# Layer 1 of a tail group by seven block products, with the last sum in two banks and the last row block's store on two queues

## The chip, the cores and the metric

The kernel runs on one core of one Trainium2 chip. The metric is device time in microseconds (us), the median of several executions. A profile is taken of one further execution; its span leaves out a little of what the timed execution counts. All runs here are with a granted TensorE clock of 0.99 or more over the span.

Two kinds of number are used. **Timed** numbers scatter: the kernel before had medians from 313.76 to 314.52 us in the rounds of these experiments, and single runs from 312.68 to 315.62, which is more than most effects here. **Positions in the profile** repeat much better once they are counted from a point that all kernels share. I count from the end of the fourth block product (code number 4) of the group before the tails, and call it **the common point**. Up to there the vector work differs slightly, but the TensorE work is the same. The page prints the span to 0.1 us; here its end is read to 0.01 from the windows view (`prof <label> --windows 305:`, whose stretch closes with the span). The recorded expectations took their ends from the page, so theirs differ from those below by up to 0.05.

## The reference

```python
def reference(q, k, v, g_ln, w_ch1, w_ch2):      # cut
    # causal attention with a window of 64, 8 batches x 8 heads x 576 rows x 64
    x = attention(q, k, v)                       # 8 x 576 x 512
    xn = (x - mean) / sqrt(var + 1e-6) * g_ln
    return x + relu(xn @ w_ch1) @ w_ch2          # 512 -> 2048 -> 512
```

The 576 rows of each batch are handled as 512 plus a tail of 64. Eight groups hold the 512-row parts; the ninth and last group collects the eight tails, 512 rows again. This last group is what the change is about.

## The kernel before

Layer 1 takes 16 blocks of hidden units, each four matmuls of 512 columns, and a relu on ScalarE (ACT):

```python
def l1(hc):
    hps = ps_mm.tile([128, 512], FP32, tag="mm", name=f"hps_{g}_{hc}")
    for kc in range(NKC):                        # 4
        nc.tensor.matmul(out=hps, lhsT=w1g[:, kc, 128 * hc:128 * (hc + 1)], rhs=zT[g][:, kc, :], ...)
    nc.scalar.activation(out=hrT[:, hc, :], in_=hps, func=AF.Relu, bias=0.0, scale=1.0)
```

Layer 2 is already done as a two by two block product with seven instead of eight products (numbers 1, 2, 6, 5, 7, 4, 3 in this order). VectorE (DVE) makes the sums S1 to S4 of layer 1's output that some of them need (`s_sums`, tile sS), and adds the finished accumulators A, B, C to the residual `x_norm` (`post`):

```python
def stage(n, p):
    product(n, p)                    # 8 matmuls of 256 columns; p = 0, 1
    if p == 0:
        return
    ...
    elif n == 7:
        post("A", 2, 1); post("C", 2, 1); post("A", 2, 0)
    elif n == 4:
        post("B", 2, 0)
        if last:
            store_rest(2, slice(0, DM), nc.sync)       # second row block, 2 x 256 KB, both on SP
    elif n == 3:
        post("C", 0, 1)
        ...
        if last:
            store_rest(0, slice(256, DM), None)        # right half of the first row block, SP and ACT
```

`store_rest` issues two transfers of 64 partitions each; with `None` one goes out on SP's queue and one on ACT's. The left half of the first row block has been stored earlier.

The softmax here doesn't subtract the row's maximum and nothing guards it: scores larger than these inputs give would overflow.

Of the kernel before, what the change touches and what calls it, by code (L numbers as in the profile page):

```python
# [10 lines left out]
FP32 = mybir.dt.float32  # L11
FP16 = mybir.dt.float16
I32 = mybir.dt.int32
RSQRT_MAGIC = float(np.frombuffer(np.uint32(0x5F3759DF).tobytes(), dtype=np.float32)[0])
AF = mybir.ActivationFunctionType
ALU = mybir.AluOpType
# [4 lines left out]
def kernel(  # L21
# [10 lines left out]
    nc = tc.nc  # L32
    B, H, S, D = q.shape
    DM = H * D
    HID = 4 * DM
    SM = 512
    NGRP = B + 1
    NKC = DM // 128
    NHC = HID // 128
# [4 lines left out]
    scale = 1.0 / (D ** 0.5)  # L44
# [3 lines left out]
    p_in = ctx.enter_context(tc.tile_pool(name="pin", bufs=2))  # L48
# [7 lines left out]
    ps_s = ctx.enter_context(tc.tile_pool(name="pss", bufs=2, space=PSUM))  # L56
    ps_x = ctx.enter_context(tc.tile_pool(name="psx", bufs=1, space=PSUM))
    ps_t = ctx.enter_context(tc.tile_pool(name="pst", bufs=1, space=PSUM))
    ps_mm = ctx.enter_context(tc.tile_pool(name="psmm", bufs=2, space=PSUM))
# [8 lines left out]
    w1g = p_const.tile([128, NKC, HID], FP16, tag="w1g", name="w1g")  # L68
# [10 lines left out]
    qk32, qk16, v32 = {}, {}, {}  # L79
    tail32, tail16, tailT, vT = {}, {}, {}, {}  # L80
    qkT, vA, vB, pts = {}, {}, {}, {}
    x_norm, zT, mvg, zsd, rstd = {}, {}, {}, {}, {}
# [300 lines left out]
    def mlp_units(g, split=0, two=False, seven=True):  # L383
        hrT = p_hrt.tile([128, NHC, 512], FP16, tag="hrT", name=f"hrT_{g}")
        hv = hrT[:, :, :].rearrange("p (c e) t -> p c e t", e=2)
# [25 lines left out]
        def add_out(kb):  # L411
            xv = x_norm[(g, kb // 2)][:, kb % 2, :]
            if g < 2:
                nc.vector.scalar_tensor_tensor(
                    out=xv, in0=ch[kb], scalar=rstd[g][:, kb:kb + 1], in1=xv, op0=ALU.mult, op1=ALU.add,
                )
            else:
                nc.vector.tensor_tensor(out=xv, in0=ch[kb], in1=xv, op=ALU.add)
            store(kb)

        def store_rest(k0, cols, eng):
            xv = x_norm[(g, k0 // 2)]
            for r in range(2):
                (eng or (nc.sync, nc.scalar)[r]).dma_start(
                    out=out[2 * k0 + r:2 * k0 + r + 3:2, SM:S, cols].rearrange("k s d -> s k d"),
                    in_=xv[64 * r:64 * r + 64, :, cols],
                )

        def store(kb):
            nc.sync.dma_start(out=out[g, 128 * kb:128 * kb + 128, :], in_=x_norm[(g, kb // 2)][:, kb % 2, :])  # L430
# [14 lines left out]
        bank = {}  # L445

        def product(n, p):
            which, a, wv = {
                1: ("A", hv[:, :, 0, 0:256], w2v[:, :, 0, 0, :]),
                2: ("B", hv[:, :, 1, 0:256], w2v[:, :, 1, 0, :]),  # L450
                6: ("A", sS[2], wT[2]),
                5: ("C", sS[1], w2v[:, :, 0, 1, :]),
                7: ("A", sS[3], wT[3]),
                4: ("B", hv[:, :, 1, 256:512], wT[4]),
                3: ("C", sS[4], w2v[:, :, 1, 1, :]),
            }[n]
            first = n in (1, 2, 5, 4)
            if p == 0 and n in (1, 2, 5):
                if which == "C":
                    bank[which] = ps_t.tile([128, 2, 256], FP32, tag="t1", name=f"p{which}_{g}")  # L460
                else:
                    bank[which] = ps_mm.tile([128, 2, 256], FP32, tag="mm", name=f"p{which}_{g}")
            for c in range(NHC // 2):
                nc.tensor.matmul(  # L464
                    out=bank[which][:, p, :], lhsT=a[:, c, 128 * p:128 * p + 128], rhs=wv[:, c, :],
                    start=(first and p == 0 and c == 0), stop=(c == NHC // 2 - 1), skip_group_check=True,
                )

        def post(which, kb0, f):
            xv = x_norm[(g, kb0 // 2)][:, :, 256 * f:256 * f + 256]  # L470
            nc.vector.tensor_tensor(out=xv, in0=bank[which], in1=xv, op=ALU.add)  # L471

        last = g == NGRP - 1

        def stage(n, p):
            product(n, p)
            if p == 0:
                return
            if n == 1:
                post("A", 0, 0)  # L480
            elif n == 2:
                post("B", 0, 0)
                if last:
                    store_rest(0, slice(0, 256), nc.sync)
            elif n == 6:
                post("A", 0, 1)
            elif n == 7:
                post("A", 2, 1)
                post("C", 2, 1)
                post("A", 2, 0)  # L490
            elif n == 4:
                post("B", 2, 0)
                if last:
                    store_rest(2, slice(0, DM), nc.sync)
                else:
                    store(2)
                    store(3)
            elif n == 3:
                post("C", 0, 1)
                tbank["shared"] = False  # L500
                tbank["n"] = 0
                if last:
                    store_rest(0, slice(256, DM), None)
                else:
                    store(0)
                    store(1)

        def l1_half(half, i):
            hps = ps_mm.tile([128, 2, 256], FP32, tag="mm", name=f"hph_{g}_{half}_{i}")
            for e in range(2):  # L510
                hc = 2 * i + e
                for kc in range(NKC):
                    nc.tensor.matmul(  # L513
                        out=hps[:, e], lhsT=w1g[:, kc, 128 * hc:128 * (hc + 1)],
                        rhs=zT[g][:, kc, 256 * half:256 * half + 256],
                        start=(kc == 0), stop=(kc == NKC - 1),
                    )
            nc.scalar.activation(out=hrT[:, 2 * i:2 * i + 2, 256 * half:256 * half + 256], in_=hps,
                                 func=AF.Relu, bias=0.0, scale=1.0)

        def l2_two(i):
            for kb in range(2):
# [9 lines left out]
                if e == NHC // 2 - 1:  # L532
                    add_out(kb)

        for half in range(2):
            for i in range(split // 2):
                units.append(lambda half=half, i=i: l1_half(half, i))
# [6 lines left out]
        if not seven:  # L544
            for kb in range(2 if two else 0, 4):
                for part in range(4):
                    units.append(lambda kb=kb, part=part: l2(kb, part))
        else:
            for n in (1, 2, 6, 5, 7, 4, 3):
                for p in range(2):  # L550
                    units.append(lambda n=n, p=p: stage(n, p))
        return units, s_sums

    def w2_sums(i, c0, c1):
        c = slice(c0, c1)
        b11, b12 = w2v[:, c, 0, 0, :], w2v[:, c, 0, 1, :]
        b21, b22 = w2v[:, c, 1, 0, :], w2v[:, c, 1, 1, :]
        t2, t3, t4 = (wT[n][:, c, :] for n in (2, 3, 4))
        o, x, y, op = {3: (t3, b22, b12, ALU.subtract), 2: (t2, t3, b11, ALU.add),
                       4: (t4, b21, t2, ALU.subtract), 1: (b12, b12, b11, ALU.subtract)}[i]  # L560
        nc.vector.tensor_tensor(out=o, in0=x, in1=y, op=op)
# [9 lines left out]
    for i in range(8):  # L571
# [7 lines left out]
        out=mask[0:64], in_=mask[0:64], compare_op=ALU.is_gt, fill=0.0,  # L579
# [3 lines left out]
        out=mask[64:128], in_=mask[64:128], compare_op=ALU.is_ge, fill=0.0,  # L583
# [14 lines left out]
    for kc in range(NKC):  # L598
        nc.tensor.matmul(out=gps[:, kc:kc + 1], lhsT=g1[:, 128 * kc:128 * kc + 128], rhs=ones1[:, 0:1],
                         start=True, stop=True)  # L600
# [61 lines left out]
    load_qk(2, 1)  # L662


    TAILS = {3: [0], 5: [1], 7: [2, 3]}
    for g in range(NGRP):
        units, s_sums = mlp_units(g, (8, 16)[g] if g < 2 else 0, g == 0, g > 1)
        slots = [[] for _ in range(len(units) + 1)]

        def at(i, f, *a):  # L670
            slots[min(i, len(slots) - 1)].append((f, a))

        b = g + 1
# [84 lines left out]
        if g > 1 and b < B:  # L758
            for j in range(4):
# [5 lines left out]
                at((12, 12, 18, 23 if b in (3, 5) else 22)[j], zt_step, b, j)  # L765
        for n, i in enumerate(TAILS.get(g, ())):
            ts = (10, 11, 14, 20) if n else (1, 2, 5, 11)
# [5 lines left out]
        n = g + 2  # L773
# [16 lines left out]
        if g > 1:  # L790
            for i in range(1, 5):
                at(7 + i, s_sums, 0, 4, i)
                at(13 + i // 3, s_sums, 4, 6, i)
                at((15, 15, 19, 21)[i - 1], s_sums, 6, 8, i)
        for n, i in enumerate(TAILS.get(g + 1, ())):
            if n == 0:
# [4 lines left out]
            else:  # L801
                at(25, load_tail, i)
        if len(TAILS.get(g, ())) == 2:
            at(3, cast_tail, TAILS[g][1])
            at(7, t_tail, TAILS[g][1], 0)
            at(8, t_tail, TAILS[g][1], 1)
        for i, u in enumerate(units):
            if g > 1 and i == 20:
                tbank["shared"] = True
            u()  # L810
            for f, a in slots[i]:
                f(*a)
# [30 lines left out]
```

## Time and profile before

| | |
|---|---|
| timed median | 313.89 us (313.62 to 314.01, 3 runs) |
| span of the profile | 313.0 us |
| common point | 279.61 us |
| last matmul ends | 307.44 us, 27.83 after the common point |
| last add ends | 308.15 us, 28.54 after it |
| end of the span | 33.38 after it, 4.84 after the last add |

The prediction below shows the chain and the windows. Two more lines: what SP's queue waited for at the end (engine and line, what it waited for, us in total, times, longest), and two of the stores whose issue falls into the stretch from 308 us on (queue, count, KB each, median us from issue to landing):

```profile
SPq L838 <- DMA out_dram<-xn: 2.7, 1, 2.7
...
out_dram<-xn SPq DMA_DIRECT2D x1, 256.0 KB, 3.6
out_dram<-xn ACTq DMA_DIRECT2D x1, 128.0 KB, 3.6
```

After its last issue SP waits another 2.7 us for the last data to land; then the program closes.

### The profile page before, as it was taken

To read this page: it belongs to the slowest core of one execution; us is meant where nothing else is said; L and a number is where in the kernel's file an instruction comes from. 1 tells how busy PE (TensorE), PEld (TensorE's weight loads), DVE (VectorE), ACT (ScalarE), POOL (GpSimd) and SP (SyncE) were. 2 spreads that over 40 slices of the span, in tenths; PEclk is the share of its full clock that TensorE was granted. 3 is DMA by queue.
4 is the path that set the end of the run, shared out by engine and by line. 5 is a ranking of instruction groups with operands and counts; after the bars stand their busy time and mean duration, and the time that the engine had idled before them with its cause. 6 is when DMAs were issued, how large, how long until landed. Compare 5 with 4: busy or idle time off the path is not lost.

```text
span 313.0 us, 7473 instructions
## 1 busy us (share of the span) xinstructions
PE 298.9 (95%) x3041; PEld 194.1 (62%) x3041; DVE 205.2 (66%) x385; ACT 153.4 (49%) x258; POOL 166.3 (53%) x251
## 2 busy tenths in 40 slices
PE   6988998899999999999999999999999999999992
PEld 4457544497554468646964686459646855784582
DVE  1689585855674996589666965896669636751642
ACT  1496633477416752776247526762475058306500
POOL 7578666454760798369814983698145506200000
PEclk9999999999999999999999999999999999999999
DMA  8999999998866996798179997993690393003013
GB/s 192 267 390 290 320 336 272 280 304 184 159 144 196 268 206 105 243 312 147 37 212 316 203 149 219 316 142 67 209 172 19 62 209 117 2 2 134 0 36 101
DMA packets 109892, 57.42 MB, mean 183 GB/s; under 512 B 79841, under 2 KB 100833, under 8 KB 109858
## 3 DMA queue, kind: packets, MB, share of 16 engines
q1 hardware_dynamic: 108944, 54.02, 69.1%
q0 software_dynamic: 768, 2.80, 3.7%
q8 instruction: 24, 0.39, 0.5%
q10 hardware_dynamic: 146, 0.13, 0.1%
q14 instruction: 10, 0.08, 0.1%
HBM read 38.80 MB, written 9.44 MB: 154 GB/s over the span
## 4 chain that ended last, share of the span: by engine, by line
PE 74%; DMA 10%; DVE 7%; SPq 4%; POOL 2%; ACT 1%; issue 1%; POOLq 0%; ACTq 0%
PE hps L392 30%; PE pA L464 11%; PE pC L464 7%; PE pB L464 7%; PE ch L404 6%; DMA w2s<-in_moe_w_ch_dram 4%; DMA qk<-in_k_dram 4%; PE xps L317 3%; PE sc L283 3%; PE hph L513 3%; PE tp L226 2%; SPq L141 2%; DVE sS L443 2%; DMA w1s<-in_moe_w_ch_dram 2%; SPq L89 1%; DVE pt L297 1%
## 5 line engine op out<-in xcount | busy, mean ns | idle before, releaser
L392 PE MATMUL hps<-zT,w1g 128*128 128x512 f16 x480 | 110.4, 379 | 0.0
L396 ACT ACTIVATE hrT<-hps 128x512 f16<-128x512 f32 x120 | 71.9, 599 | 50.7 <-PE hps L392 47.2
L392 PEld LDWEIGHTS <-w1g 128*128 128x128 f16 x480 | 44.6, 98 | 49.3 <-issue 1.0
L290 ACT ACTIVATE pt<-sc 128x512 f16<-128x512 f32 x72 | 39.0, 595 | 29.8 <-DVE xn L471 15.6
L464 PEld LDWEIGHTS <-sS 128*128 128x128 f16 x448 | 43.3, 98 | 5.1
L342 POOL TENSOR_SCALAR rsz<-mvg 128x1 f32<-128x1 f32 x28 | 10.7, 382 | 60.4 <-DVE mvg L328 59.8
L128 POOL CAST qk<-qk 128x1024 f16<-128x1024 f32 x32 | 35.1, 1112 | 13.4 <-DMA qk<-in_q_dram 6.9
L464 PEld LDWEIGHTS <-hrT 128*128 128x128 f16 x336 | 32.6, 98 | 5.2
L212 ACT COPY qkT<-tp 128x1024 f16<-128x1024 f16 x16 | 16.1, 1012 | 35.2 <-PE tp L226 26.1
L297 DVE TENSOR_TENSOR pt<-pt,mask 128x1024 f16<-128x1024 f16 x32 | 25.4, 800 | 11.9 <-ACT pt L290 11.9
L471 DVE TENSOR_TENSOR xn<-pA,xn 128x512 f32<-128x512 f32 x28 | 19.2, 686 | 21.1 <-PE pA L464 21.1
L443 DVE TENSOR_TENSOR sS<-hrT 128x512 f16<-128x512 f16 (+1 forms) x42 | 24.8, 591 | 10.2 <-ACT hrT L396 10.2
L464 PE MATMUL pA<-wT,sS 128*128 128x256 f16 x224 | 26.9, 273 | 0.0
L345 POOL TENSOR_SCALAR z<-xn,rsz 128x512 f16<-128x512 f32 x28 | 25.3, 902 | 2.9
L464 PE MATMUL pC<-w2s,sS 128*128 128x256 f16 x224 | 26.8, 273 | 0.0
L325 DVE BATCH_NORM_STATS2 stats<-xn 128x6 f32<-128x512 f32 x36 | 25.0, 695 | 1.2
L323 DVE TENSOR_TENSOR xn<-xps,rcp 128x512 f32<-128x512 f32 x36 | 24.9, 692 | 1.2
L513 PE MATMUL hph<-zT,w1g 128*128 128x256 f16 x192 | 23.2, 272 | 2.3 <-ACT zT L360 1.1
L320 DVE RECIPROCAL rcp<-xps 128x8 f32<-128x8 f32 x36 | 7.4, 205 | 26.8 <-PE xps L317 26.8
L404 PE MATMUL ch<-w2s,hrT 128*128 128x512 f16 x96 | 23.1, 380 | 0.0
L513 PEld LDWEIGHTS <-w1g 128*128 128x128 f16 x192 | 18.3, 98 | 5.1 <-issue 2.6
L317 PEld LDWEIGHTS <-pt 128*64 128x64 f16 x576 | 12.2, 110 | 14.4 <-issue 6.4
(85 smaller groups left out, 395.1 us busy)
## 6 DMA issues: line engine op xcount, KB each, us to landing
out_dram<-xn SPq DMA_DIRECT2D x34, 256.0 KB, 2.6
qk<-in_q_dram SPq DMA_DIRECT2D x16, 512.0 KB, 6.2
qk<-in_k_dram SPq DMA_DIRECT2D x16, 512.0 KB, 7.4
v<-in_v_dram SPq DMA_DIRECT2D x32, 256.0 KB, 6.5
w2s<-in_moe_w_ch_dram SPq DMA_DIRECT2D x12, 512.0 KB, 5.7
w1s<-in_moe_w_ch_dram SPq DMA_DIRECT2D x4, 512.0 KB, 6.7
tk<-in_k_dram SPq DMA_DIRECT2D x8, 256.0 KB, 4.7
tv<-in_v_dram SPq DMA_DIRECT2D x8, 256.0 KB, 5.3
```

The source lines that it names most:

```text
L128: nc.gpsimd.tensor_copy(out=dst[:, :].rearrange("p (a j) e d -> p a e j d", j=j), in_=t[:, :].rearrange("p (a e j d) -> p a e j d", e=2, j ...
L290: nc.scalar.activation(out=o, in_=i, func=AF.Exp, bias=0.0, scale=scale)
L297: nc.vector.tensor_tensor(out=ptv, in0=ptv, in1=mb, op=ALU.mult)
L323: nc.vector.tensor_tensor(out=xn, in0=xps[:, :, 0:D], in1=rcp_b, op=ALU.mult)
L325: nc.vector.bn_stats(out=stats, in_=xv)
L345: nc.gpsimd.tensor_scalar(out=z, in0=xv, scalar1=rs, scalar2=nm, op0=ALU.mult, op1=ALU.add)
L392: nc.tensor.matmul(out=hps, lhsT=w1g[:, kc, 128 * hc:128 * (hc + 1)], rhs=zT[g][:, kc, :], start=(kc == 0), stop=(kc == NKC - 1),)
L396: nc.scalar.activation(out=hrT[:, hc, :], in_=hps, func=AF.Relu, bias=0.0, scale=1.0)
L404: nc.tensor.matmul(out=ch[kb], lhsT=hrT[:, hc, 128 * kb:128 * (kb + 1)], rhs=w2s[:, hc, :], start=(hc == 0), stop=(hc == NHC - 1),)
L443: nc.vector.tensor_tensor(out=o, in0=x, in1=y, op=op)
L464: nc.tensor.matmul(out=bank[which][:, p, :], lhsT=a[:, c, 128 * p:128 * p + 128], rhs=wv[:, c, :], start=(first and p == 0 and c == 0), st ...
L513: nc.tensor.matmul(out=hps[:, e], lhsT=w1g[:, kc, 128 * hc:128 * (hc + 1)], rhs=zT[g][:, kc, 256 * half:256 * half + 256], start=(kc == 0) ...
```

## The change

The intent: do layer 1 of the last group with seven block products too. Its inputs are cut in two along the contraction and in two along the rows, its weights accordingly; four sums of weight blocks (`w1S`) and four of activation blocks (`zsums`) are made on VectorE in the group before. For each of four blocks of hidden units, products 1, 6, 7, 4 go into one accumulator A, 2 into B, 5 and 3 into C. A and C are read between products:

```diff
+        def l1_a(d):
+            l1_product(1, d)
+            l1_keep("s1", "A", d)                      # ACT copies A
+            l1_product(2, d)
+            l1_sum(l1_quad(d, 0, 0), "B", "s1", d)     # DVE: B + s1; relu on POOL
+            l1_product(5, d)
+            l1_keep("s5", "C", d)
+        def l1_b(d):
+            l1_product(6, d)
+            l1_keep("u2", "A", d)
+            l1_product(3, d)
+            l1_sum(l1_quad(d, 0, 1), "C", "u2", d)     # DVE: C + u2, relu on DVE
+        def l1_c(d):
+            l1_product(7, d)
+            l1_sum(l1_quad(d, 1, 1), "A", "s5", d)     # DVE: A + s5, relu on DVE
+        def l1_e(d):
+            l1_product(4, d)                           # relu of A on ACT
...
+                for d in range(1, 4):
+                    l1_a(d)
+                    l1_c(d - 1)
+                    l1_b(d)
+                    l1_e(d - 1)
+                s_sums(0, 4)
+                stage(1, 0)
+                l1_c(3)
+                s_sums(0, 4, 1)
+                s_sums(4, 8, 1)
+                stage(1, 1)
+                l1_e(3)
+                s_sums(0, 4, 2)
+                stage(2, 0)
...
```

At the end, the last sum (accumulator C of layer 2) gets a bank of accumulator memory (PSUM) for each half, and the second row block's store is spread over the two queues:

```diff
+                    for r in range(2):
+                        bank[("C", r)] = ps_t.tile([128, 256], FP32, tag=f"t{r}", name=f"pC{r}_{g}")
...
+            if last and n == 3:
+                post_c(0, p)                           # 256 elements instead of 512
+                if p:
+                    store_rest(0, slice(256, DM), None)
+                return
...
-                    store_rest(2, slice(0, DM), nc.sync)
+                    store_rest(2, slice(0, DM), None)
```

More of the change, by code (lines that the diff above doesn't have):

```diff
@@ L458, in product @@
             if p == 0 and n in (1, 2, 5):
-                if which == "C":
+                if which == "C" and last:
+                    for r in range(2):
+                        bank[("C", r)] = ps_t.tile([128, 256], FP32, tag=f"t{r}", name=f"pC{r}_{g}")
+                elif which == "C":
                     bank[which] = ps_t.tile([128, 2, 256], FP32, tag="t1", name=f"p{which}_{g}")
@@ L462, in product @@
                     bank[which] = ps_mm.tile([128, 2, 256], FP32, tag="mm", name=f"p{which}_{g}")
+            split_c = last and which == "C"
+            o = bank[(which, p)][:, :] if split_c else bank[which][:, p, :]
             for c in range(NHC // 2):
                 nc.tensor.matmul(
-                    out=bank[which][:, p, :], lhsT=a[:, c, 128 * p:128 * p + 128], rhs=wv[:, c, :],
-                    start=(first and p == 0 and c == 0), stop=(c == NHC // 2 - 1), skip_group_check=True,
+                    out=o, lhsT=a[:, c, 128 * p:128 * p + 128], rhs=wv[:, c, :],
+                    start=(first and (p == 0 or split_c) and c == 0), stop=(c == NHC // 2 - 1), skip_group_check=True,
                 )
@@ L471, in post, with post_c @@
             nc.vector.tensor_tensor(out=xv, in0=bank[which], in1=xv, op=ALU.add)
+        def post_c(kb0, r):
+            xv = x_norm[(g, kb0 // 2)][:, r, 256:512]
+            nc.vector.tensor_tensor(out=xv, in0=bank[("C", r)], in1=xv, op=ALU.add)
         last = g == NGRP - 1
@@ L488, in stage @@
                 post("A", 2, 1)
-                post("C", 2, 1)
+                if last:
+                    post_c(2, 0)
+                    post_c(2, 1)
+                else:
+                    post("C", 2, 1)
                 post("A", 2, 0)
@@ L501, in stage @@
                 tbank["n"] = 0
-                if last:
-                    store_rest(0, slice(256, DM), None)
-                else:
-                    store(0)
-                    store(1)
+                store(0)
+                store(1)
         def l1_half(half, i):
@@ L533, in l2_two, with l1_product @@
                     add_out(kb)
+        lbank = {}
+        def l1_product(n, d):
+            w1v = w1g[:, :, :].rearrange("p (a k) (i e m) -> p a k i e m", a=2, e=2, m=128)
+            t1, t2, t3, t4 = (zS["sum"][:, m] for m in range(4))
+            z = zT[g]
+            which, a, b = {
+                1: ("A", w1v[:, 0, :, :, 0, :], z[:, 0:2, 0:256]),
+                2: ("B", w1v[:, 1, :, :, 0, :], z[:, 2:4, 0:256]),
+                5: ("C", w1S[1], t1),
+                6: ("A", w1S[2], t2),
+                3: ("C", w1S[4], z[:, 2:4, 256:512]),
+                7: ("A", w1S[3], t3),
+                4: ("A", w1v[:, 1, :, :, 1, :], t4),
+            }[n]
+            if n == 1:
+                pool, tag = (ps_mm, "mm") if d == 2 else (ps_s, "sc")
+                lbank[("A", d)] = pool.tile([128, 2, 256], FP32, tag=tag, name=f"lA_{d}")
+            elif n == 2:
+                lbank[("B", d)] = ps_t.tile([128, 2, 256], FP32, tag="t0", name=f"lB_{d}")
+            elif n == 5:
+                if d % 2:
+                    lbank[("C", d)] = ps_t.tile([128, 2, 256], FP32, tag="t1", name=f"lC_{d}")
+                else:
+                    lbank[("C", d)] = ps_x.tile([128, 4, 256], FP32, tag="xps", name=f"lC_{d}")[:, 0:2]
+            o = lbank[(which, d)]
+            for r in range(2):
+                for kc in range(2):
+                    nc.tensor.matmul(
+                        out=o[:, r, :], lhsT=a[:, kc, 2 * d + r, :], rhs=b[:, kc, :],
+                        start=(n in (1, 2, 5) and r == 0 and kc == 0), stop=(kc == 1), skip_group_check=True,
+                    )
@@ new lines, in l1_quad, with l1_part, l1_keep, l1_sum @@
+        def l1_quad(d, e, h):
+            return hv[:, 2 * d:2 * d + 2, e, 256 * h:256 * h + 256]
+        def l1_part(x, d):
+            return zS[x][:, d % 2, :].rearrange("p (r t) -> p r t", r=2)
+        def l1_keep(x, which, d):
+            nc.scalar.copy(out=l1_part(x, d), in_=lbank[(which, d)])
+        def l1_sum(o, which, x, d):
+            nc.vector.tensor_tensor(out=o, in0=lbank[(which, d)], in1=l1_part(x, d), op=ALU.add)
+            eng = nc.gpsimd if x == "s1" else nc.vector
+            eng.tensor_scalar(out=o, in0=o, scalar1=0.0, scalar2=None, op0=ALU.max)
@@ new lines, in l1_e, with plan @@
+        def l1_e(d):
+            l1_product(4, d)
+            nc.scalar.activation(out=l1_quad(d, 1, 0), in_=lbank[("A", d)], func=AF.Relu, bias=0.0, scale=1.0)
+        if last:
+            def plan():
+                yield
+                l1_b(0)
+                for d in range(1, 4):
[12 more added lines that the diff above has]
+                stage(2, 0)
+                s_sums(4, 8, 2)
+                stage(2, 1)
+                stage(6, 0)
+                s_sums(0, 4, 3)
+                stage(6, 1)
+                s_sums(4, 8, 3)
+                stage(5, 0)
+                s_sums(0, 4, 4)
+                stage(5, 1)
+                s_sums(4, 8, 4)
+                for n in (7, 4, 3):
+                    for p in range(2):
+                        stage(n, p)
+                yield
+            l1_a(0)
+            return plan(), s_sums
@@ L552, in mlp_units, with w1_sums, z_sums @@
         return units, s_sums
+    w1S = {}
+    def w1_sums(*which):
+        wv = w1g[:, :, :].rearrange("p (a k) (i e m) -> p a k i e m", a=2, e=2, m=128)
+        a11, a12, a21, a22 = (wv[:, b, :, :, a, :] for a, b in ((0, 0), (0, 1), (1, 0), (1, 1)))
+        for n in which:
+            w1S[n] = p_in.tile([128, NKC // 2, NHC // 2, 128], FP16, tag=f"qk32_{n % 2}", name=f"w1S{n}")
+            o = w1S[n][:, :, :, :]
+            x, y, op = {1: (a21, a22, ALU.add), 2: (w1S.get(1), a11, ALU.subtract),
+                        3: (a11, a21, ALU.subtract), 4: (a12, w1S.get(2), ALU.subtract)}[n]
+            nc.vector.tensor_tensor(out=o, in0=x, in1=y, op=op)
+    zS = {}
+    def z_sums(g, *which):
+        if not zS:
+            t = p_in.tile([128, 4, 512], FP32, tag="v32", name="zsums", bufs=1)
+            zS["s5"] = t[:, 2:4, :]
+            zS["s1"] = p_in.tile([128, 2, 512], FP32, tag="tk32", name="s1sums", bufs=1)
+            zS["u2"] = p_in.tile([128, 2, 512], FP32, tag="tv32", name="u2sums", bufs=1)
+            zS["sum"] = t[:, 0:2, :].rearrange("p a n -> p (a n)").bitcast(FP16).rearrange(
+                "p (n k t) -> p n k t", n=4, k=2)
+        b11, b12 = zT[g][:, 0:2, 0:256], zT[g][:, 0:2, 256:512]
+        b21, b22 = zT[g][:, 2:4, 0:256], zT[g][:, 2:4, 256:512]
+        t1, t2, t3, t4 = (zS["sum"][:, n] for n in range(4))
+        for n in which:
+            o, x, y = {1: (t1, b12, b11), 2: (t2, b22, t1), 3: (t3, b22, b12), 4: (t4, b21, t2)}[n]
+            nc.vector.tensor_tensor(out=o, in0=x, in1=y, op=ALU.subtract)
     def w2_sums(i, c0, c1):
@@ L662, with begin_last @@
     load_qk(2, 1)
+    def begin_last():
+        nonlocal rest
+        rest, _ = mlp_units(NGRP - 1)
+        next(rest)
+    rest = None
     TAILS = {3: [0], 5: [1], 7: [2, 3]}
     for g in range(NGRP):
+        if g == NGRP - 1:
+            for _ in rest:
+                pass
+            break
         units, s_sums = mlp_units(g, (8, 16)[g] if g < 2 else 0, g == 0, g > 1)
@@ L806 @@
             at(8, t_tail, TAILS[g][1], 1)
+        if g == NGRP - 2:
+            at(0, w1_sums, 1, 2)
+            at(3, w1_sums, 3)
+            at(21, w1_sums, 4)
+            at(24, z_sums, NGRP - 1, 1, 2)
+            at(25, z_sums, NGRP - 1, 3, 4)
+            at(27, begin_last)
         for i, u in enumerate(units):
```

## The prediction

> **What bounds the kernel now.** I read the page's busy shares first, then the chain of work that ended last, in order of time, then the windows of the last stages, then their timeline. The busy shares say which engine to watch:
>
> ```profile
> span 313.0 us, 7473 instructions
> PE 298.9 (95%) x3041; PEld 194.1 (62%) x3041; DVE 205.2 (66%) x385; ACT 153.4 (49%) x258; POOL 166.3 (53%) x251
> ```
>
> PE is busy 95% of the span, but the change touches only the last group (the tails) and a few vector instructions in the group before it, so the average decides nothing. The chain from 281 us on does:
>
> ```profile
> 281.35 13.84 PE hps L392 x64
> 295.19 1.75 PE pA L464 x16
> ...
> 305.68 1.76 PE pC L464 x16
> 307.44 0.02 issue
> 307.46 0.69 DVE xn L471
> ```
>
> These are start, length, engine, tile and line. Nothing but matmuls is on the chain: layer 1 of the tails takes 13.84 us for 64 products of 512 columns (216 ns each), each block product of layer 2 takes 1.75 us for 16 of 256 columns (109 ns each), back to back, until one vector add closes it. The windows of layer 1, layer 2 and the tail after the last matmul (busy time and instructions of each engine, then clock, DMA share, GB/s):
>
> ```profile
> 281.20:295.00 13.80, 13.80 (x66) 6.22 (x64) 4.80 (x9) 8.96 (x15) 0.00 (x0) 1.00 0.21 77
> 295.00:307.45 12.45, 12.42 (x113) 10.87 (x111) 6.26 (x11) 0.60 (x1) 0.00 (x0) 1.00 0.10 22
> 307.45:313.00 5.55, 0.00 (x0) 0.00 (x0) 0.69 (x1) 0.00 (x0) 0.00 (x0) 0.93 0.55 142
> ```
>
> PE has no gap in the first two rows; DVE has 4.80 of 13.80 us in use, ACT 8.96, POOL none. So a cut of PE work here is worth its full time, as long as the evacuations keep up. The third row is 5.55 us in which only the last add and the stores run. In the timeline:
>
> ```profile
> 306.16 0.69 DVE L471 TENSOR_TENSOR xn<-pB,xn 128x512 f32<-128x512 f32 x1
> 306.88 1.98 SPq L424 DMA_DIRECT2D out_dram<-xn  x3
> 307.46 0.69 DVE L471 TENSOR_TENSOR xn<-pC,xn 128x512 f32<-128x512 f32 x1 [0.61 <-PE pC L464]
> 308.18 0.70 ACTq L424 DMA_DIRECT2D out_dram<-xn  x1
> ```
>
> SP issues three stores in a row, 0.66 us each: both halves of the second row block (256 KB each) at 306.88 and about 307.5, then half of the last one.
>
> **What the Trainium skill says.** "TensorE: Matmul & The Clock Gate", section "Back-to-back issue gap", gives N/2.4 + 2.5 ns when warm: 215.8 ns for 512 columns and 109.2 for 256. The chain has 216 and 109, so it agrees, and halving the width costs only 1.3 ns a matmul. "VectorE: DVE Perf Modes", section "The perf-mode tier table", lets tensor_tensor run at double rate on 16-bit SBUF operands and at single rate with PSUM, and a 16-bit tensor_scalar in SBUF at four times. The trace agrees with the first two: 512 elements from PSUM take 0.69 us and 1024 f16 elements from SBUF 0.69 as well; no row of before shows the third in f16. "PSUM — Partial Sum Buffer", section "PSUM bank collisions raise a hardware error", says that engines must not touch one bank at the same time in the same partitions. That is why the change gives the two halves of the last sum a bank each: the first can be added while PE fills the second. "DMA: Bandwidth & Descriptors", section "Issuing engines are not separate DMA queues", says that a second issuing engine saves issue time alone. Here that is one 0.6 us issue, for the second row block.
>
> **The change, part by part.**
>
> *PE, removed and added.* 64 matmuls of 512 columns go: 13.84 us. In come 7 products x 4 blocks x 4 matmuls = 112 of 256 columns: 112 x 0.109 = 12.2 us. Gain 1.63 us if PE never waits.
>
> *Preparation in the group before.* DVE gets four sums of weights, 128x2048 f16. By the pace of the sums there (successive independent ones start 0.34 us apart for 512 elements, 0.61 for 1024) I estimate 1.15 us each, and four sums of the activations at 0.34 each. They go where DVE sat idle: the timeline has it idle for 2.64 us before the mask at 255.52, 2.13 us before 258.34, and 2.54 us before 277.97. Two weight sums end at about 255.3, the third at 257.4, the fourth with two activation sums at about 277.4. Cost on the path: 0.
>
> *Layer 1 with waits.* The order of instructions shows each accumulator A and C being read between products: A collects products 1, 6, 7, 4 of a block, with a copy by ACT after 1 and 6, an add by DVE after 7 and a relu by ACT after 4. I lay one block out, PE starting it at 0, in the order 1, 2, 5, 7 (of the block before), 6, 3, 4 (of the block before), 0.437 us each, 3.06 in all. A reader starts 0.20 us after the last issue (a 256-column matmul lasts 0.273, spaced 0.109, plus 0.04 from the end of a matmul to its reader); PE starts again 0.07 after its releaser (seen at 263.32). ACT copies product 1 at 0.74-1.34 (0.60 by the row of hrT). DVE adds product 2 to it at 1.37-2.06. Product 7 was issued by 1.75, so its add could start at 1.95 but gets DVE at 1.98 and ends at 2.67. Product 4 could go at 2.62 and goes at 2.74: a wait of 0.12. Everything else has slack: ACT has 4 x 0.6 = 2.4 us of 3.2, DVE 3 adds and 2 relus, about 2.6. Four such blocks, one of them with less: about 0.42 us of waits.
>
> *The seam to layer 2.* The relu on ACT after the last product 4 ends 0.8 us after its issue, but layer 2's product 2 wants it as weights 0.66 us later, and a weight load that comes late costs 0.07 + 0.21 (the distance of weight load and first matmul at 294.82): wait 0.41. Then DVE has to do, after the last block's add: relu 0.2, two sums S1 at 0.61, the first post add 0.61, two sums S2. These sums used to be made in pieces while layer 1 ran; now their second halves need the last block. The first S2 half comes 0.29 us late for product 6, the second 0.16 later: 0.45. After that DVE catches up during product 5.
>
> *The end.* The last add handles 256 elements instead of 512: 0.69 becomes about 0.42, gain 0.27. The second row block's stores go out on SP and ACT together and earlier, so that they have largely drained when the last ones come. The last ACT store took 3.6 us to landing against 2.5 for the quiet 128 KB stores earlier: of these 1.1 us I count 0.2 as gained, because all three stores together still take about 3.2 us of transfer.
>
> Sum: -1.63 + 0.42 + 0.41 + 0.45 - 0.27 - 0.20 = **-0.82 us**, so 313.89 becomes about 313.1.
>
> **The rivals.** First, *PE keeps its whole gain*: ACT and DVE are quicker than laid out, or the waits fall into the same gaps. For it: both have slack on average. Against it: product 4 hangs on two successive DVE adds in every block. It gives -1.63 - 0.27 - 0.2 = -2.1: 311.8. Second, *DVE becomes the bound of layer 1*: if the f16 relu is at single rate (0.6 us) or waits for POOL's relu beside it, DVE has 3 x 0.65 + 2 x 0.6 = 3.2 us for a block, and the lateness adds up at the seam. Against it: the wait that matters comes before the relu. It gives 1.0 to 1.5 us more than my sum: 314.1 to 314.6. Third, *the end is paced by the transfers*: 0.79 MB moved in 3.2 us at the end, so the time follows the start of the second block's stores, which come both at once instead of 0.6 us apart and after an earlier add. That would make the store worth up to 0.8 rather than 0.2: 312.5. Fourth, *the weight sums delay the attention of the group before*: two sums end only 0.2 us before the mask; if they are slower, some tenths are added, at most 0.5.
>
> **Range and chances.** The largest conceivable gain, 2.1 us and the store's rest, is under 0.9% of 313.89; the losses that I can name come to under 2 us in all. Two per cent would be 6.3 us, which nothing here reaches. The chances are 0.01, 0.98 and 0.01. For the time, the first and third rival pull down, the second and fourth up; I leave the middle at 313.1 with 312.1 to 314.2.
>
> **What would show it.** Right: 112 new matmuls in about 12.7 us from their first to the last with layer 2's first product taken out, PE idle some 0.1 us before each product 4, a wait of about 0.4 us at layer 2's product 2 and as much at product 6, both on ACT and DVE; last matmul 0.3 us earlier; last add 0.4 us long. Wrong: idle PE before products 6 or 3 (ACT is the bound), a DVE relu of 0.5 us or more, an idle PE in the group before, or last stores landing at the same 3.6 us.

## The result, and the profile after

The changed kernel takes 313.11 us (313.05 to 313.54, 4 runs) against 313.76 for the kernel before in the same rounds. The ratio is 0.9981, interval 0.9964 to 0.9999. Ratios here are the mean time of one kernel's runs over the mean of the other's in the same rounds, so they are not quite the ratio of the medians quoted.

The predicted 313.1 is thus met. But the profile shows that two parts of the sum were off in opposite directions, layer 1 by 0.26 us and the end by 0.57. Counted from the common point, which lies at 278.35 us here:

| us | before | changed | difference | predicted |
|---|---|---|---|---|
| last matmul ends | 27.83 | 27.22 | -0.61 | -0.35 |
| last add, from there | 0.71 | 0.45 | -0.26 | -0.27 |
| end of the span, from there | 4.84 | 5.20 | +0.36 | -0.20 |
| sum | 33.38 | 32.87 | -0.51 | -0.82 |

The page of the changed kernel begins so:

```profile
span 311.2 us, 7625 instructions
PE 298.5 (96%) x3089; PEld 198.1 (64%) x3089; DVE 217.8 (70%) x411; ACT 153.1 (49%) x258; POOL 171.4 (55%) x255
```

The span is 1.8 us shorter than before, but 1.26 us of that is the earlier common point, which the change has no part in. VectorE has 12.6 us more to do, and the windows show how close it now runs. The three stretches are layer 1 from its second block step on, layer 2, and the tail (columns as in the prediction):

```profile
281.40:294.35 12.95, 12.95 (x119) 11.30 (x117) 10.63 (x21) 7.43 (x13) 5.23 (x4) 1.00 0.18 66
294.35:305.57 11.22, 10.99 (x96) 8.90 (x94) 9.44 (x17) 0.60 (x1) 0.00 (x0) 1.00 0.12 26
305.57:311.20 5.63, 0.00 (x0) 0.00 (x0) 0.42 (x1) 0.00 (x0) 0.00 (x0) 0.77 0.55 140
```

DVE is busy for 10.63 of 12.95 us where it had been for 4.80 of 13.80. In layer 2 PE's busy time falls short of the stretch for the first time, by 0.23 us, and that is not all its waiting: a matmul lasts 0.273 us and the next one starts 0.109 us after it, so a pause of up to 0.16 us leaves no gap. The chain in order of time shows the waits as longer pieces:

```profile
287.59 0.45 PE lC L578 x4
288.04 0.93 PE lA L578 x8
288.97 0.44 PE lB L578 x4
...
291.17 0.49 PE lA L578 x4
...
293.01 0.70 DVE hrT L593
...
293.74 0.29 DVE hrT L595
294.03 0.66 DVE sS L443 x2
...
296.49 2.09 PE pA L469 x16
...
303.81 1.76 PE pC L469 x16
...
305.60 0.42 DVE xn L480
```

Four products are 0.44 us and eight 0.87, so the 0.93 at 288.04 holds a wait of 0.06 before the block's product 4, and the 0.49 at 291.17 one of 0.05. From 293.01 to 296.44 the chain leaves PE and goes through VectorE: the last block's add and relu, then sums. Product 6 of layer 2 (pA at 296.49) then takes 2.09 instead of the usual 1.91 from first start to last end. The waits at this seam, from the view of who waited for whom, with PEld the weight loads:

```profile
PEld L469 <- DVE sS L443: 0.7, 2, 0.5
PEld L469 <- ACT hrT L617: 0.3, 1, 0.3
PE pA L469 <- DVE sS L443: 0.2, 1, 0.2
```

The sum of PE's waits follows from the time: 27.22 us, less 112 matmuls of layer 1 at 0.109 us and eight block products of 1.745 us, leaves about 1.0 us. (Eight, since product 3 of the group before falls behind the common point.) By pieces: the blocks 0.07, 0.06, 0.05 and 0.07; product 2 of layer 2, 0.21 (its matmuls span 2.12 instead of 1.91 us); product 6, 0.35 before it and 0.18 in it.

The end in the timeline, for comparison with the four lines in the prediction:

```profile
304.90 0.41 DVE L480 TENSOR_TENSOR xn<-pC,xn 128x256 f32<-128x256 f32 x1
305.01 1.91 ACTq L424 DMA_DIRECT2D out_dram<-xn  x2
305.60 0.42 DVE L480 TENSOR_TENSOR xn<-pC,xn 128x256 f32<-128x256 f32 x1 [0.28 <-PE pC L469]
```

The first half of the last sum is added while PE fills the second, as meant. Yet SP's final wait is longer, not shorter, and so is the landing of ACT's stores:

```profile
SPq L1003 <- DMA out_dram<-xn: 3.2, 1, 3.2
...
out_dram<-xn ACTq DMA_DIRECT2D x1, 256.0 KB, 4.4
...
out_dram<-xn ACTq DMA_DIRECT2D x1, 128.0 KB, 4.1
```

So the end gave back what the last add had gained. Why, and what layer 1 is worth alone, is what the experiments are for.

### The profile page after: what moved, and what is told of

The parts are those of the page before. It is cut to its first block, busy times and chain, and to the rows that moved or that the text cites. A ratio compares the mean times of both kernels' runs of the same rounds, so it can differ in the third digit from the quotient of the medians.

```text
span 311.2 us, 7625 instructions
## 1 busy us (share of the span) xinstructions
PE 298.5 (96%) x3089; PEld 198.1 (64%) x3089; DVE 217.8 (70%) x411; ACT 153.1 (49%) x258; POOL 171.4 (55%) x255
## 4 chain that ended last, share of the span: by engine, by line
PE 74%; DMA 10%; DVE 6%; SPq 3%; POOL 2%; issue 1%; ACT 1%; POOLq 0%; ACTq 0%
PE hps L392 25%; PE pA L469 10%; PE pC L469 7%; PE pB L469 7%; PE ch L404 7%; DMA qk<-in_q_dram 4%; DMA w2s<-in_moe_w_ch_dram 4%; PE hph L528 3%; PE xps L317 3%; PE sc L283 3%; DVE sS L443 2%; PE lA L578 2%; PE tp L226 2%; SPq L141 2%; DMA w1s<-in_moe_w_ch_dram 2%
## 5 line engine op out<-in xcount | busy, mean ns | idle before, releaser
L392 PE MATMUL hps<-zT,w1g 128*128 128x512 f16 x416 | 96.4, 380 | 0.0
L396 ACT ACTIVATE hrT<-hps 128x512 f16<-128x512 f32 x104 | 62.3, 599 | 38.6 <-PE hps L392 35.1
L392 PEld LDWEIGHTS <-w1g 128*128 128x128 f16 x416 | 38.3, 98 | 42.0 <-issue 0.9
L528 PEld LDWEIGHTS <-w1g 128*128 128x128 f16 x192 | 18.1, 97 | 4.6 <-issue 2.0
```

The source lines that it names most:

```text
L528: nc.tensor.matmul(out=hps[:, e], lhsT=w1g[:, kc, 128 * hc:128 * (hc + 1)], rhs=zT[g][:, kc, 256 * half:256 * half + 256], start=(kc == 0) ...
```

## The experiments

Ten kernels ran, all correct. What they tell lies in their positions after the common point, from one profile each (for e9 the last add stands for the useless instruction behind it):

| run | last matmul | last add ends | end | tail behind the add | timed median (before) | ratio, interval |
|---|---|---|---|---|---|---|
| before | 27.83 | 28.54 | 33.38 | 4.84 | | |
| changed | 27.22 | 27.67 | 32.87 | 5.20 | 313.11 (313.76) | 0.9981, 0.9964 to 0.9999 |
| e1_store_sp | 27.22 | 27.66 | 33.15 | 5.49 | 314.01 (314.52) | 0.9986, 0.9963 to 1.0009 |
| e2_split_only | 27.83 | 28.28 | 33.85 | 5.57 | 314.96 (314.52) | 1.0016, 0.9992 to 1.0040 |
| e3_layer1_only | 27.22 | 27.94 | 32.74 | 4.80 | 313.15 (314.52) | 0.9962, 0.9939 to 0.9985 |
| e4_early_sums | 26.71 | 27.15 | 32.38 | 5.23 | 313.75 (314.52) | 0.9977, 0.9943 to 1.0011 |
| e5_cols | 26.70 | 27.15 | 31.62 | 4.47 | 311.77 (313.97) | 0.9934, 0.9908 to 0.9959 |
| e6_cols_one_add | 26.71 | 27.42 | 31.69 | 4.27 | 311.69 (313.97) | 0.9937, 0.9911 to 0.9964 |
| e7_seam_cols | 26.50 | 26.95 | 31.43 | 4.48 | 311.55 (313.97) | 0.9929, 0.9904 to 0.9954 |
| e8_before_cols | 27.82 | 28.54 | 32.68 | 4.14 | 313.32 (313.97) | 0.9978, 0.9949 to 1.0007 |
| e9_split_delayed | 27.83 | 28.75 | 33.42 | 4.67 | 313.65 (313.93) | 0.9994, 0.9974 to 1.0014 |
| e10_final_rows | 26.50 | 26.94 | 31.71 | 4.77 | 312.45 (313.93) | 0.9953, 0.9933 to 0.9973 |

### e1_store_sp: the second block's store back on SP alone

```diff
 # on the changed kernel
-                    store_rest(2, slice(0, DM), None)
+                    store_rest(2, slice(0, DM), nc.sync)
```

> The changed kernel with one thing undone: the second row block's two 256 KB stores go out on SP alone again, one after the other. Measured from the end of the fourth product of the group before the tails (the last common point; 33.39 us to the end of the span in the kernel before, 32.86 in the changed one). Theory A: the store on two queues lost 0.33 us, because the ACT queue's first store delays its last one; then this run is 0.3 to 0.4 us shorter than the changed kernel, about 32.5, and the last ACT store lands after 3.6 us instead of 4.1. Rival B: the end is paced by the transfers of 0.79 MB that begin with the second block's first store, whatever queue issues them; then nothing is gained, 32.8 to 33.2. My prediction said the two queues are worth 0.2 us, so that this run would be 0.2 longer, 33.06.

It ends at 33.15, 0.28 later than the changed kernel. Theory A falls: the store on two queues does not cost 0.33, it is worth 0.28, close to the 0.20 that I had predicted for it. Then the loss must come with the other part of the end.

### e2_split_only: the last add by halves, alone

The edit puts the `bank[("C", r)]`, `post_c` and `n == 3` lines of the change into the kernel before; layer 1 and the stores stay.

> The kernel before with one part of the change: the last sum's two halves in a bank each, added by 256 elements; layer 1 and the stores stay. Theory A (the chain goes through the last add): the last add takes 0.42 instead of 0.69 us and the span from the common point falls by 0.27, to 33.1. Rival B (paced by the transfers that begin with the second block's store, which this does not move): 33.3 to 33.4, no gain.

Neither theory held. The last add ends 0.26 us earlier than before, as it should, and the end comes 0.47 **later**, 33.85. The timed ratio of 1.0016 leans the same way without being clear of 1. The timeline shows what moved:

```profile
305.93 1.98 SPq L424 DMA_DIRECT2D out_dram<-xn  x3
306.45 0.43 DVE L480 TENSOR_TENSOR xn<-pC,xn 128x256 f32<-128x256 f32 x1 [0.22 <-PE pC L469]
306.91 0.70 ACTq L424 DMA_DIRECT2D out_dram<-xn  x1
```

SP issues three stores back to back, 0.66 us each, so its last one cannot go out before 305.93 + 1.32 = 307.25, however early the add is done. Only ACT's last store moves ahead, to 306.91: 28.31 after the common point instead of 28.57. It takes 4.0 us to land instead of 3.6, and SP's last wait is 3.1 instead of 2.7.

### e3_layer1_only: layer 1 alone

The edit undoes the two banks, the two adds and the store on two queues in the changed kernel.

> The changed kernel with the end undone: one bank for the last sum, one add of 512, second block's store on SP alone; only layer 1 by seven products stays. Both theories: the last matmul ends 27.2 us after the common point (27.83 in the kernel before, 27.23 in the changed one), the span is 32.8 (33.39 less 0.60), so layer 1 alone would give the whole gain, the end nothing. If the end was worth what I predicted (0.47), it is 33.3.

The last matmul ends at 27.22, to 0.01 us where the changed kernel has it, and the end comes at 32.74, 0.13 **earlier** than in the changed kernel. So layer 1 is the whole gain of the change, and the rest of the change takes a little away. In the timed runs, too, layer 1 alone has the better ratio (0.9962), but the intervals overlap.

### e4_early_sums: the sums for layer 2 in VectorE's gaps

```diff
                 for d in range(1, 4):
+                    if d > 1:
+                        s_sums(2 * d - 4, 2 * d - 2, 1)
                     l1_a(d)
...
-                s_sums(0, 4)
                 stage(1, 0)
+                s_sums(0, 4, 2)
                 l1_c(3)
-                s_sums(0, 4, 1)
                 s_sums(4, 8, 1)
                 stage(1, 1)
                 l1_e(3)
-                s_sums(0, 4, 2)
                 stage(2, 0)
```

> The changed kernel with the S1 sums of the first blocks moved into VectorE's idle gaps in layer 1 and half of S2 before the last block's add. The theory that the wait before layer 2's product 6 (0.53 us in the changed kernel) is VectorE's queue of sums at the seam: product 6 starts without a wait and the last matmul ends 0.4 to 0.5 us earlier, 26.7 to 26.8 after the common point, the span 32.3 to 32.5. Rival: VectorE has no room and the sums delay the adds on which product 4 hangs; then the waits in the blocks grow by what the seam loses, 27.2.

The last matmul ends at 26.71, 0.51 earlier, and the end comes at 32.38. In the chain, product 6 follows product 2 without a gap:

```profile
295.60 1.26 PE pB L469 x10
296.86 1.75 PE pA L469 x16
```

The wait of 0.53 us before product 6 was VectorE's queue of sums at the seam: S1 of the first blocks stood behind the last block's add although its inputs had long been there. The timed runs of this kernel scatter from 312.11 to 315.51, and settle nothing by themselves.

### e5_cols and e6_cols_one_add: half of the second block's store earlier

```diff
                     post_c(2, 0)
                     post_c(2, 1)
+                    store_rest(2, slice(256, DM), None)
...
-                    store_rest(2, slice(0, DM), None)
+                    store_rest(2, slice(0, 256), None)
```

> The kernel with the early sums, and in addition the second row block stored in two column halves: the right half as soon as its two adds are done (about 1.4 us earlier than the whole), the left half after the last add to it. Theory B (the end follows the start of the second block's store by about 5 us of transfers and 1.2 us of closing): half of the 512 KB is out of the way, and from the end of the last add to the end of the span it is 4.3 to 4.8 us instead of 5.25; from the common point 31.5 to 32.0 instead of 32.4. Theory A (the end is a fixed latency of the last store behind the last add): no change, 32.3 to 32.5.

> As the run with column halves, but with the last sum in one bank and one add of 512 again. With the transfers out of the way the last add should now count: 0.27 us longer from the common point than the run with column halves. If the transfers still pace the end, the two are the same within 0.1.

The column halves end at 31.62, 0.76 earlier than e4, with PE and the last add unmoved: theory B, the transfers pace the end. The second run, with one add of 512, ends its add 0.27 later and the whole only 0.07 later, inside the 0.1 of its second case. So even here most of the split's gain is lost: ACT's last store goes out 0.27 later, but lands in 2.8 us instead of 3.0. The first store of the same size on that queue takes 2.8 in both.

### e7_seam_cols: another order of the last block

The edit, shortened:

```diff
 # after the loop, in place of l1_b(3) ... stage(1, 1), l1_e(3), stage(2, 0)
+                l1_product(6, 3); l1_keep("u2", "A", 3); l1_product(3, 3)
+                # C + u2 on DVE, without relu
+                l1_e(2)
+                l1_product(7, 3)
+                # A + s5 on DVE, then both relus on DVE
+                stage(1, 0)
+                l1_e(3)
+                s_sums(4, 8, 1)
+                s_sums(0, 4, 2)
+                stage(1, 1)
+                stage(2, 0)
```

> As the run with column halves, with the last block's products in another order: product 7 before layer 2's product 1, product 4 between its halves, and the last two relus on VectorE after both adds. The wait before layer 2's product 2 (0.21 us) and that before the last product 4 (0.06) should go: last matmul 26.45 to 26.6 after the common point instead of 26.71, span shorter by 0.15 to 0.25 than the run with column halves. If VectorE is late with the add after product 7, product 4 waits 0.2 to 0.4 instead and nothing is gained.

The last matmul ends at 26.50, as expected, and the chain has full-rate products from the second half of layer 2's product 1 on:

```profile
293.35 0.51 PE lA L579 x4
293.86 0.87 PE pA L469 x8
294.73 1.75 PE pB L469 x16
296.48 1.75 PE pA L469 x16
```

The last product 4 still waits 0.07. The end comes 0.19 earlier, nearly all of the 0.20 that PE gains. This kernel has the lowest median of all: 311.55 us against 313.97, ratio 0.9929, interval 0.9904 to 0.9954; the ratios of e5 and e6 lie within that interval.

### e8_before_cols: the kernel before, with nothing but column halves

```diff
                 post("C", 2, 1)
+                if last:
+                    store_rest(2, slice(256, DM), None)
                 post("A", 2, 0)
...
-                    store_rest(2, slice(0, DM), nc.sync)
+                    store_rest(2, slice(0, 256), None)
```

> The kernel before with nothing changed but the second row block's store: two column halves on both queues, the right one earlier. Theory B: with PE and the last add as they were (27.83 and 28.54 after the common point) the end comes 0.4 to 0.9 us earlier, 32.5 to 33.0 instead of 33.39. Theory A (fixed latency behind the last add): 33.3 to 33.4.

The first half goes out at 25.88 after the common point, 1.39 before the whole store of the kernel before, and the last add keeps its length:

```profile
305.20 3.30 SPq L424 DMA_DIRECT2D out_dram<-xn  x3
307.18 0.69 DVE L471 TENSOR_TENSOR xn<-pC,xn 128x512 f32<-128x512 f32 x1 [0.61 <-PE pC L464]
```

With the last matmul and the last add where they were before, the end comes at 32.68 instead of 33.38: 0.70 us for three lines, more than the whole change brought in its profile. These lines also bring in the second queue, which e1 puts at 0.28 in the changed kernel; e5 has it on both sides, and there the halves alone are worth 0.76. Its timed ratio, 0.9978, is in line with that, but the interval reaches 1.0007. The other runs fit: in the seven profiles that store the second block whole, the end comes 6.1 to 6.5 us after the first issue of that store (26.66 after the common point and 32.87 in the changed kernel, for one), while the tail behind the last add varies from 4.67 to 5.57.

### e9_split_delayed: a useless instruction ahead of the last stores

```diff
 # on e2_split_only
                 post_c(0, p)
                 if p:
+                    xv = x_norm[(g, 0)][:, :, 256:512]
+                    nc.vector.tensor_scalar(out=xv, in0=xv, scalar1=1.0, scalar2=None, op0=ALU.mult)
                     store_rest(0, slice(256, DM), None)
```

> The kernel before with the last sum in two banks, as in the run of the split alone, but a useless multiplication by one (about 0.35 us on VectorE) between the last add and the last stores, so that these are issued as late as in the kernel before (about 28.65 us after the common point). In the run of the split alone the ACT store was issued 0.26 us earlier than before and the end came 0.41 us later (33.80 against 33.39). Theory: a last store that is issued while the second block's transfers still wait is slowed and slows them; then the useless instruction brings the end back to 33.3 to 33.5, earlier than without it. Rival: it is something else in the split (or chance in the stores), then the end is 33.8 or later, up to 34.2.

ACT's last store is issued 0.47 us later than in the split alone (28.78 against 28.31 after the common point), SP's 0.10, and the end comes at 33.42, 0.43 **earlier**. In the timeline, and SP's last wait:

```profile
307.32 0.43 DVE L490 TENSOR_SCALAR xn<-xn 128x512 f32<-128x512 f32 x1
307.78 0.70 ACTq L424 DMA_DIRECT2D out_dram<-xn  x1
...
SPq L858 <- DMA out_dram<-xn: 2.6, 1, 2.6
```

ACT's store lands in 3.5 us again, and SP waits 2.6. With the two banks and the narrower add still in place, the loss is gone, so in these profiles it was the moment of issue that did it. The timed ratios, 0.9994 here and 1.0016 for the split alone, point the same way, with intervals that overlap. The packets in the trace show where most of it goes. From the first packet of these stores to the last, in the split alone and here (the last three columns are the clock, the DMA share and GB/s):

```profile
307.17:310.78 3.61, 0.00 (x0) 0.00 (x0) 0.00 (x0) 0.00 (x0) 0.00 (x0) 1.00 0.88 218
307.58:310.90 3.32, 0.00 (x0) 0.00 (x0) 0.16 (x1) 0.00 (x0) 0.00 (x0) 0.70 0.91 237
```

The same 0.79 MB takes 0.29 us longer in the split alone. There the first packet on ACT's queue comes at 30.61 after the common point instead of 31.14, while SP's queue still moves the second block, and SP's last packet ends at 32.18 instead of 31.70. The other kernels that store the second block whole fit this: 3.36 us before and in e3, 3.5 to 3.6 in e1, e4 and the changed kernel, whose last store also goes out early (in the latter two both queues carry the second block as well). Why the packets take longer when both queues have work stays open.

### e10_final_rows: the last store in row halves

```diff
 # on e7_seam_cols
                 post_c(0, p)
-                if p:
-                    store_rest(0, slice(256, DM), None)
+                for r in range(2):
+                    (nc.sync, nc.scalar)[r].dma_start(out=out[r + 2 * p, SM:S, 256:DM],
+                        in_=x_norm[(g, 0)][64 * r:64 * r + 64, p, 256:DM])
```

> The fastest kernel so far (product order at the seam and column halves) with the very last store in two row halves, the first issued right after its own add, 0.7 us before the last. Theory that the last transfers pace the end: 128 KB instead of 256 KB after the last add, the span from the common point 31.1 to 31.3 instead of 31.48. Rival: two more issues of 0.6 to 0.7 us on queues that are busy (SP and ACT each have three in 3.05 us) put the last issue off by 0.2 to 0.3 us: 31.5 to 31.8.

It ends at 31.71, 0.28 later than e7: the rival held. The first row half's add ended at 305.31, but both queues were still issuing the second block's left half until about 305.6, so the row halves all went out from 305.70 on, one after the other:

```profile
305.70 1.20 SPq L489 DMA_DIRECT2D out_dram<-xn  x2
305.75 1.46 ACTq L489 DMA_DIRECT2D out_dram<-xn  x2
```

Half the data after the last add did not pay for one more issue on each queue.

## Why the prediction was right or wrong

The number was right, and the picture of layer 1 was. The step "the end" was half wrong, and two wrong terms partly cancelled. That the time fell on 313.1 to 0.01 us is luck besides: the interval of the ratio allows a gain of 0.03 to 1.1 us, and the kernel before stood at 313.76 in these rounds, not at the 313.89 from which the prediction counted.

**PE removed and added: right.** 112 matmuls ran at 0.109 us where nothing held them; what the formula of "TensorE: Matmul & The Clock Gate", section "Back-to-back issue gap", gives for 256 columns (109.2 ns) held in layer 1 as in layer 2. The prediction left out that the page gives it for an isolated matmul and puts a stream with weight loads at about 131 ns for 512 columns; the stream of 64 in the kernel before took 216, so here the formula holds and the 131 does not.

**Preparation in the group before: right.** The weight sums took 1.22 us each and lay in the gaps named. From the start of the last add of the group before that to the common point it was 279.61 - 252.19 = 27.42 us before and 278.35 - 250.92 = 27.43 after: no cost.

**Layer 1's waits: right in place, too large.** The wait falls before product 4 of each block, behind two successive adds of VectorE, with nothing before product 6 and at most 0.02 us before product 3. It is 0.05 to 0.07 us a block, 0.25 in all, where I had 0.42. In the last step of the loop, counted from its first matmul as in the prediction, ACT's copy of product 1 ran from 0.69 to 1.27 (I had 0.74 to 1.34), and product 4 started at 2.69 instead of 2.74. One term in the working was off the other way without harm: I had put VectorE's f16 relu at 0.2 us, and it took 0.294. The rival that VectorE bounds layer 1 did not come: that relu took half of the 0.6 us that the rival needs, and it lies behind the add that counts.

**The seam: right in kind, the shares swapped.** Product 2's wait for the relu on ACT was 0.21 instead of 0.41; product 6's wait for the S2 sums was 0.53 instead of 0.45. e4 shows that the latter is the order of VectorE's queue, and e7 that the former goes with the order of the last block's products. In all, PE's waits took 1.0 of the possible 1.63 us; I had said 1.28.

**The end: here the prediction failed.** The step said: "The last add handles 256 elements instead of 512: 0.69 becomes about 0.42, gain 0.27." The add did become 0.42, but the time did not follow: e2 shows the end 0.47 later by it. I treated the chain's last add as what sets the end, and the stores as an addition to it. The step about the store, 0.2 us gained by two queues, was right by itself (e1: 0.28). Together these parts cost 0.13 us (changed kernel against e3) where I had 0.47 gained. The prediction's own sign of being wrong came too: ACT's last store landed not faster than in 3.6 us, but in 4.1.

My third rival, that the end is paced by the transfers, is what e5 and e8 show. I had put the weight on it wrongly: it does not make the given change better, since the whole store still starts only after the last add to that block. It makes a change better that moves half of it ahead. Once that is done the transfers hold the end less: ACT's last store lands in 2.8 us in e6 and e8, like the first on that queue.

The sum: layer 1 brought 0.26 us more than predicted and the end 0.57 less, which leaves -0.51 in the profile where I had -0.82; the timed medians have -0.65. A right total with two wrong terms, so the total alone would have taught nothing.

## What to carry to other kernels

When a chain ends in a vector add and a store, ask which transfers are still in flight when the last store goes out: here moving half of the previous store 1.4 us forward was worth 0.7 to 0.8 us (in the smaller case together with a second queue), and shortening the last add was worth nothing or less. A block product with fewer matmuls pays what its evacuations leave: lay out the order of the vector engine's queue at the seam to the next stage, since a sum that is ready can stand behind one that is not. And for effects of a few tenths of a microsecond, compare positions from a common point in the profile before trusting medians, which lay up to 0.8 us apart for one and the same kernel.

## What the Trainium skill lacked or had wrong

- "DMA: Bandwidth & Descriptors", section "Issuing engines are not separate DMA queues", says that a second issuing engine saves issue time alone. The store on two queues was worth 0.28 us (e1 against the changed kernel), less than the one issue of 0.6 us that it saves, which agrees. The section also says that the transfers interleave, but the page has no figure for what that costs a last store: issued about 0.5 us earlier on ACT's queue, while the block before it was still being stored, it made the same 0.79 MB take 3.61 us instead of 3.32 and the end come 0.43 us later (e2 against e9).
- "GPSIMD Engine Reference", section "Elementwise — side-by-side cycle accounting", names 769 ns measured for 512 elements in a tight loop as the best case. The in-place f16 relu of 512 elements on POOL took 1484 to 1497 ns, about twice as long, while a scaling from f32 to f16 of the same size takes 0.76 us at its shortest and 0.90 on average in the kernel before. VectorE worked beside each of the four relus, so no run here shows it alone. It cost nothing here, since the result is needed later. The page gives no figure for f16 in place.
- "VectorE: DVE Perf Modes", section "The TRN2 errata", has both a formula with a fixed 58 cycles and the remark that about 150 cycles are measured. For the f16 tensor_scalar of 512 elements at four per cycle I estimate 0.19 us from the first and 0.29 from the second; the runs show 0.293 to 0.295, so the remark is right and the formula is not.
